# A decode layer with its gradients: the first V window on ScalarE's queue, K windows in slots of their own, the last fill in nested DMAs

## The chip, the core and the metric

The kernel runs on one core of a Trainium2 chip. The metric is the device time of one execution in microseconds; for each kernel the median of its runs is given. Beside the times there is one profiled execution, with a record of every instruction and of every DMA packet. The engines are called by their names or as the profile has them: PE (TensorE), DVE (VectorE), ACT (ScalarE), POOL (GpSimd) and SP (SyncE, which only issues DMAs here). Sixteen DMA engines carry all transfers of the core.

## The reference

One token goes through a pre-norm attention block with a sliding window over a cache and through a bilinear MLP, and then all gradients are taken:

```python
h  = x + attention(layernorm(x), k_cache[..., Sk-W:, :], v_cache[..., Sk-W:, :], wq, wo)
h2 = h + (g * u) @ w_down        # g, u = layernorm(h) @ w_gate, layernorm(h) @ w_up
out, vjp = jax.vjp(f, x, k_cache, v_cache, wq, wo, w_gate, w_up, w_down)
return (out, *vjp(grad_out))
```

Sizes: D = 448, 16 query heads over G = 8 groups of keys and values, head size 256, F = 1792, cache length Sk = 32768, of which the last W = 4096 positions are used. Everything is bfloat16. The gradients of the two caches have the shape of the caches (134 MB each): outside the window they are zero, and these zeros have to be written. That makes 280.59 MB written and 48.33 MB read in one execution.

## The kernel before, in words

The work has three streams.

**Zeros, on SP's queue.** `zeros` is a tile of 128 rows. Sixteen of its rows (`ALL`, rows 32, 36, ..., 92) are the source of every fill, so that each of the sixteen belongs to another DMA engine. `fill` writes a region of HBM from these rows over and over; each descriptor is one row piece of f elements, ZW = 8192 (16 KB) or, for the regions counted in `LONG`, NW = 14336 (28 KB). At first `zeros` holds wq, which the queries need; the first fill therefore comes from another zeroed tile (`odd`, part of `Mt`), and once the queries are done a DMA on ScalarE's queue writes zeros into the sixteen rows (line 110). Then SP issues one fill after another without looking at the compute: regions (0,0) to (7,0) of the two cache gradients (`zero_rows_and_fills`, line 108). The last region, `out_3` of group 7, is cut up by `deal`, which gives some engines more than others: `deal(FILL, 0, 3, 14)` gives 14 pieces of 16 KB to each of the first three rows, `deal_all` gives all sixteen rows the same, and `deal_rest` gives further pieces to POOL's queue in two laps, the first after the forward pass, the second after the last results.

**Loads and results, on POOL's queue.** `BIG` is one tile with nine slots of 16 KB per partition and a tail. A window of K or V of one group (2 MB) fills a slot. V of group g lies in slot g; K goes to slots 7 and 8 in turn (`K_SLOT`). `io_load` keeps the loads in the order in which the program writes them, one behind the other. At the start K0, V0, K1, V1 and V2 are issued; K of group g + 2 is loaded in two halves when group g is done, and V7 in two halves into the slot of K6. The rows x and grad_out (0.9 KB each) come by ScalarE's queue into the first partition of slot 6.

**Compute.** For each group, `scores` (line 363) transposes K on PE by eight tiles of PSUM, copies each to SBUF (`products`, line 346, with `evac`, which takes ScalarE and VectorE in turn) and multiplies by q; `softmax` follows; `moments` (line 393) forms the products of the window that the backward pass needs. The scores of group g + 1 are woven into the moments of group g. After the eight groups come wo, the MLP and its gradients, with the weights loaded by the same queue over the K slots, then `dq` and its broadcast rows. The last stage walks over the eight groups once more, and computes the window's gradients of K and V from small products (line 764), evicts them from PSUM (lines 298 and 300) into a pair of slots, and POOL issues two stores of 2 MB per group (line 789). Behind the last of these come the small pieces of `deal_rest(1)`.

`rows_to_half` (line 231) turns a row of 448 numbers into a tile over partitions by seven casts and small matmuls. `to_rows` (line 561) does the opposite for the rows that are broadcast into `bc2` and `dq_bc`.

Of the kernel before, what the change touches and what calls it, by code (L numbers as in the profile page):

```python
# [8 lines left out]
f32 = mybir.dt.float32  # L9
# [27 lines left out]
TAIL = 9 * SLOT  # L37
RING = TAIL + 6016
SIZE = RING
K_SLOT = [KS + g % 2 for g in range(G)]  # L40


@with_exitstack
def kernel(
# [10 lines left out]

    oT_f = const.tile([128, 32], f32)
    BIG = const.tile([128, SIZE], bf16)
    x_bf = BIG[0:1, 6 * SLOT:6 * SLOT + D]
    S_.dma_start(out=x_bf, in_=A_x.rearrange("a b d -> (a b) d"))
    go_bf = BIG[0:1, 6 * SLOT + 512:6 * SLOT + 512 + D]  # L60
    S_.dma_start(out=go_bf, in_=grad_out.rearrange("a b d -> (a b) d"))

    def flat_rows(w):
# [39 lines left out]
        fill(FILL, last[used[0]:used[0] + 16 * n * f], ALL, n, f)  # L103
        used[0] += 16 * n * f

    LONG = range(6, 11)

    def zero_rows_and_fills():
        f = NW // 4
        S_.dma_start(out=zeros[ALL, :].rearrange("p (n f) -> p n f", f=f), in_=odd[ALL, 0:f].unsqueeze(1).to_broadcast([16, 4, f]))  # L110
        fill(FILL, first[16 * NH * FH:], ALL, (FL - NH * FH) // ZW, ZW)
        for g in range(G):
            for k, o in enumerate((out_2, out_3)):
                if (g, k) not in ((0, 0), (G - 1, 1)):
                    f = NW if 2 * g + k in LONG else ZW
                    fill(FILL, region(o, g), ALL, FL // f, f)
        deal(FILL, 0, 3, 14)
        deal_all(24, ZW)
        deal_all(8, 1224)

    def deal_rest(lap):
        if lap == 0:
            deal(IO, 0, 4, 16, ZL)
            deal(IO, 4, 3, 4, ZL)
            deal(IO, 7, 2, 25, ZL)
            deal(IO, 9, 7, 10, ZL)
        else:
            deal(IO, 0, 5, 2, 512)
            deal(IO, 5, 2, 25)
            deal(IO, 7, 2, 2, 2560)  # L130
            deal(IO, 9, 7, 15)
            assert used[0] == 896 * ZW

    def slot(k):
# [35 lines left out]
    def load_V(g):  # L170
        load_window(Vw[g], A_v_cache, g)

    def load_V_half(g, h):
        t = slice(h * T // 2, (h + 1) * T // 2)
        io_load(Vw[g][:, t, :], A_v_cache[0, g, Sk - W:, :].rearrange("(p t) d -> p t d", t=T)[:, t, :])

    load_K(0)
    load_V(0)
    load_K(1)
    load_V(1)  # L180
    wd_rows = B_w_down.rearrange("(s j m) n -> j s (m n)", s=2, j=128)
    load_V(2)


    ident_bf = const.tile([128, 128], bf16)
# [42 lines left out]
        r0, r1 = i // 2, (7 + i) // 2  # L228
        return row.rearrange("o (m r) -> o m r", r=NI)[:, :, r0:r1 + 1:r1 - r0]

    def rows_to_half(row):
        t = ps.tile([128, NI], f32, tag="tmp", bufs=1)
        for i in range(NI):
            xe = small.tile([1, 128], f32, tag="R", name="xe")
            c = xe[:]
            V_.tensor_copy(out=c.rearrange("o (m r) -> o m r", r=2), in_=half_cols(row, i))  # L236
            P_.matmul(t[:, i:i + 1], lhsT=c, rhs=one[0:1, 0:1], start=True, stop=True)  # L237
        return t

# [56 lines left out]
    def evac(out, in_):  # L296
# [3 lines left out]
            V_.tensor_copy(out=out, in_=in_)  # L300
        evac_ctr[0] += 1

    xX = const.tile([128, NI], f32)
    V_.tensor_copy(out=xX[:], in_=rows_to_half(x_bf)[:])
    rstd1, xh1, xf1, xx1 = layernorm(xX[:], "ln1")


# [35 lines left out]
        pk_ctr[0] += 1  # L343
        return ring(k).rearrange("p (i h d) -> p i h d", i=2, h=2)

    def products(pool, x_at, vecT, g, out_ps, q):
        tr = pool.tile([128, 4, 2, 128], bf16, tag="tr", bufs=2, name="tr")
        for i in range(4):
            for dh in range(2):
                P_.transpose(tr[:, i, dh, :], x_at(g, 4 * q + i)[:, dh * 128:(dh + 1) * 128], ident_bf[:])  # L350
        xt = kt_buf()
        evac(xt, tr[:])
        for i in range(4):
            for dh in range(2):
                P_.matmul(out_ps[:, 4 * q + i, :], lhsT=xt[:, i, dh, :], rhs=vecT[:, 4 * g + dh:4 * g + dh + 3:2],  # L355
                          start=(dh == 0), stop=(dh == 1))
# [6 lines left out]
    def scores(g, q):  # L363
        if q == 0:
            sT[g] = fps.tile([128, T, 2], f32, tag="sT", bufs=2, name="sT")
        products(fps, k_at, qT, g, sT[g], q)

    def softmax(g):
        s = sT[g]
        pmax = small.tile([128, 2], f32, tag="pmax")  # L370
        V_.reduce_max(out=pmax[:], in_=s[:].rearrange("p t h -> p h t"), axis=AX)
        mt = ps.tile([2, 128], f32, tag="tmp", bufs=1)
        P_.transpose(mt[:], pmax[:], ident_f[:])
        gmax = small.tile([2, 1], f32, tag="gmax")
        V_.reduce_max(out=gmax[:], in_=mt[:], axis=AX)
        gd = small.tile([2, 2], f32, tag="gd")
        V_.tensor_scalar(out=gd[:], in0=ident_f[0:2, 0:2], scalar1=gmax[:, 0:1], scalar2=-SCALE, op0=ALU.mult, op1=ALU.mult)
        nb = ps.tile([128, 2], f32, tag="tmp", bufs=1)
        P_.matmul(nb[:], lhsT=one[0:2, 0:1].to_broadcast([2, 128]), rhs=gd[:], start=True, stop=True)
        nbias = small.tile([128, 2], f32, tag="nbias")  # L380
        V_.tensor_copy(out=nbias[:], in_=nb[:])
        e = small.tile([128, T, 2], f32, tag="ef")
        sums = small.tile([128, 2], f32, tag="psums")
        for h in range(2):
            S_.activation(out=e[:, :, h], in_=s[:, :, h], func=ACT.Exp, bias=nbias[:, h:h + 1], scale=SCALE, accum_out=sums[:, h:h + 1])
        rs = small.tile([128, 2], f32, tag="rsum")
        V_.reciprocal(out=rs[:], in_=total(sums[:], 2)[:])
        pf = small.tile([128, T, 2], f32, tag="pp", bufs=2)
        V_.tensor_tensor(out=pf[:], in0=e[:], in1=rs[:].unsqueeze(1).to_broadcast([128, T, 2]), op=ALU.mult)
        V_.tensor_copy(out=pT_all[:, g], in_=pf[:])  # L390
        p_f[g] = pf

    def moments(g):

# [3 lines left out]
        for c in range(T // 2):  # L398
# [16 lines left out]
            if g + 1 < G and 4 <= c < 12:  # L415
                with tc.issue_after(mm.ins):
                    scores(g + 1, c - 4)
                if c == 11:
                    softmax(g + 1)
            if c == 8 and g == G - 2:  # L420
                load_V_half(G - 1, 0)
            if c == 8 and g == G - 1:
                load_wo(0, 9)
        S_.copy(out=Mt[:, g, 0, :], in_=MT[0][:])
# [29 lines left out]

    bc2 = [BIG[:, o:o + F].rearrange("p (i c) -> p i c", i=2) for o in (WD0, WD0 - F)]

    for q in range(8):
        scores(0, q)
    softmax(0)
    for g in range(G):  # L460
        moments(g)
        if g + 2 < G:
            load_K(g + 2, 2)
        if g + 3 < G - 1:
            load_V(g + 3)
        if g == G - 2:
            load_V_half(G - 1, 1)
        if g == 0:

            go_f = BIG[0:1, 6 * SLOT + 1024:6 * SLOT + 1024 + 2 * D].bitcast(f32)  # L470
            V_.tensor_copy(out=go_f, in_=go_bf)
            t = ps.tile([128, D], f32, tag="tmp", bufs=1)
            P_.matmul(t[:], lhsT=one[0:1, 0:1].to_broadcast([1, 128]), rhs=go_f, start=True, stop=True)
            S_.copy(out=dh2_bc[:], in_=t[:])
    load_wo(9, 32)
    io_load(wg_sb, flat_rows(B_w_gate))

# [80 lines left out]
    for w in range(2):  # L558
        V_.tensor_tensor(out=dgu[:, w, 0:FC], in0=d_hh[:], in1=gu[:, 1 - w, :], op=ALU.mult)

    def to_rows(dst, t, cols, j0):
        for j, c in enumerate(cols):
            P_.matmul(t[:, j, :], lhsT=c, rhs=ident_bf[:, j0:j0 + t.shape[-1]], start=True, stop=True)
        evac(dst, t)

    P2 = const.tile([128, 2, NI], f32)
    for w, w_sb in ((0, wg_sb), (1, wu_sb)):
        for h in range(4):
            r = small.tile([2, HF // 4], bf16, tag="R", name="r")
            t = ps.tile([2, NI, 32], f32, tag="tmp", bufs=1, name="t")  # L570
            to_rows(r[:].rearrange("s (j m) -> s m j", m=NI), t[:], [dgu[:, w, m::NI] for m in range(NI)], 32 * h)
            for i2 in range(2):
                bc = ps.tile([128, HF // 4], f32, tag="tmp", bufs=1, name="bc")
                P_.matmul(bc[:], lhsT=Par[:, i2:i2 + 128], rhs=r[:], start=True, stop=True)
                evac(bc2[w][:, i2, h * HF // 4:(h + 1) * HF // 4], bc[:])
        wv = w_sb.rearrange("p (i c) -> p i c", i=NI)
        for i in range(NI):
            V_.tensor_tensor_reduce(out=wv[:, i, :], in0=wv[:, i, :], in1=bc2[w][:, i % 2, :], scale=1.0, scalar=0.0,
                                    op0=ALU.mult, op1=ALU.add, accum_out=P2[:, w, i:i + 1])
    dhn = const.tile([128, NI], f32)  # L580
# [7 lines left out]
    for b in range(32):  # L588
        V_.tensor_tensor_reduce(out=wg_sb[:, 0:D], in0=parked.get(b, wo_b(b)), in1=dh_bc[:], scale=1.0, scalar=0.0,  # L589
                                op0=ALU.mult, op1=ALU.add, accum_out=doW[:, b:b + 1])  # L590
    doT_f = small.tile([128, 32], f32, tag="pp", bufs=2, name="doT_f")
    V_.tensor_copy(out=doT_f[:], in_=regroup(doW[:], 1)[:])
    doT = const.tile([128, 32], bf16)
# [25 lines left out]
    rows16(doT, do_rows, 1.0)  # L619
    for b1 in range(0, 16, 4):  # L620
        r = wg_sb[0:2, b1 * 128:b1 * 128 + 512]
        t = ps.tile([2, 4, 128], f32, tag="tmp", bufs=1, name="t")
        to_rows(r.rearrange("s (b c) -> s b c", c=128), t[:], [dq[:, b:b + 17:16] for b in range(b1, b1 + 4)], 0)
        for i2 in range(2):
            bc = ps.tile([128, 512], f32, tag="tmp", bufs=1, name="bc")
            P_.matmul(bc[:], lhsT=Par[:, i2:i2 + 128], rhs=r, start=True, stop=True)
            evac(dq_bc[:, i2, b1 * 128:b1 * 128 + 512], bc[:])
    load_odd(IO)
# [92 lines left out]
    def dP(s, q):  # L721
        g = SEQ[s]
        if q == 0:
            dps[s] = bps.tile([128, T, 2], f32, tag="dp", name="dp")
        products(bps, v_at, doT, g, dps[s], q)

    def factors(s):
        R_ps = ps.tile([128, 2 * Dh], f32, tag="tmp", bufs=1)
# [94 lines left out]
```

## Time and profile before

| what | value |
|---|---|
| median of 3 runs | 777.7 us (776.77 to 778.44) |
| profiled execution | 777.6 us, its span 775.8 us |
| PE busy | 468.8 us (60%) |
| VectorE busy | 394.3 us (51%) |
| ScalarE busy | 155.5 us (20%) |
| POOL busy | 42.2 us (5%) |
| mean granted TensorE clock | 0.665 |
| moved by DMA | 330.09 MB |

Busy shares of compute engines are averages over the span. The span is also cut into 40 equal slices of 19.4 us, with a digit for the busy share in tenths, and a line for the DMA engines together. DMA queues are listed by the bytes they moved and by the share of the sixteen engines' time that their packets took. A view by stretches gives, for any cut of the span, each engine's busy time with the number of instructions, the granted clock, the DMA share and GB/s. The DMA share can pass 1 by a little, since packets overlap by a few nanoseconds.

The stages lie like this: the first scores from 18 us, the moments of the eight groups from 41 to 246 us, some 26 us each; wo and the MLP to 335; gradients of the MLP to 407; the last stage to 702.

### The profile page before, as it was taken

Reading aid. Unit: us, or ns where it says so; the run is one execution under the profiler, and the core shown is the slowest. Engines: PE = TensorE matmul, PEld = TensorE weight load, DVE = VectorE, ACT = ScalarE, POOL = GpSimd, SP = SyncE. Lnnn points to the kernel's source line nnn. Section 1 sums busy time; section 2 is a strip of 40 time slices with the busy share of each in tenths; the row PEclk is TensorE's granted clock in tenths of the full one; section 3 lists DMA queues with packets and bytes.
Section 4 is the critical chain, followed back from the end, with each engine's and each line's share of the span. In section 5 each row is a group of like instructions: output and inputs, shape, how many; then the busy total and the mean of one; then the engine's idle time right before and its main releaser. Section 6 shows DMA issues by size and latency. Waiting matters only on the chain. (4 is left out here: it accounts for less than half of the span.)

```text
span 775.8 us, 10948 instructions
## 1 busy us (share of the span) xinstructions
PE 468.8 (60%) x4427; PEld 259.6 (33%) x4472; DVE 394.3 (51%) x1179; ACT 155.5 (20%) x268; POOL 42.2 (5%) x86
## 2 busy tenths in 40 slices
PE   3899998998996423041326839686958977360000
PEld 2755565555553121020323414232313333030000
DVE  5277766766774121146683526464646756980000
ACT  0211222122110000021003414243423433130000
POOL 2000000000000000010001000000000100001000
PEclk9999999999999755555555555555555555555555
DMA  9999999999999999999999999999999999999998
GB/s 362 429 426 429 425 427 429 427 425 427 428 424 429 433 428 430 436 437 430 427 432 428 431 428 433 428 429 424 432 430 429 431 428 429 429 430 432 431 429 349
DMA packets 22803, 330.09 MB, mean 425 GB/s; under 512 B 2717, under 2 KB 2719, under 8 KB 3992
## 3 DMA queue, kind: packets, MB, share of 16 engines
q1 hardware_dynamic: 12701, 231.17, 69.6%
q0 software_dynamic: 9968, 97.77, 29.9%
q8 instruction: 35, 0.57, 0.3%
q10 hardware_dynamic: 84, 0.46, 0.1%
q14 instruction: 15, 0.12, 0.0%
HBM read 48.33 MB, written 280.59 MB: 424 GB/s over the span
## 5 line engine op out<-in xcount | busy, mean ns | idle before, releaser
L764 PE MATMUL d_ps<-BIG 32*128 32x512 bf16 x256 | 121.4, 598 | 60.2 <-ACT BIG L298 42.8
L407 PE MATMUL MT<-BIG 128*128 128x512 bf16 x467 | 134.5, 394 | 3.8 <-DMA BIG<-in_A_v_cache_dram 1.9
L403 DVE TENSOR_SCALAR BIG<-BIG,pf 128x256 bf16<-128x256 bf16 x512 | 112.6, 280 | 29.9 <-PE MT L407 25.2
L350 PE MATMUL tr<-ident_bf,BIG 128*128 128x128 bf16 x1024 | 113.5, 269 | 20.1 <-DVE doW L589 12.6
L298 ACT CAST BIG<-d_ps 128x512 bf16<-128x512 f32 x156 | 88.4, 588 | 176.8 <-PE d_ps L764 128.3
L350 PEld LDWEIGHTS <-BIG 128*128 128x128 bf16 x1024 | 81.1, 120 | 51.9 <-issue 44.1
L300 DVE COPY BIG<-tr 128x1024 bf16<-128x1024 bf16 x92 | 63.3, 688 | 50.7 <-PE tr L350 50.6
L300 DVE CAST BIG<-d_ps 128x512 bf16<-128x512 f32 x100 | 67.9, 683 | 34.8 <-DMA out_dram<-BIG 28.1
L298 ACT COPY BIG<-tr 128x1024 bf16<-128x1024 bf16 x36 | 36.4, 1012 | 131.6 <-PE tr L350 116.3
L355 PEld LDWEIGHTS <-BIG 128*128 128x128 bf16 x1024 | 36.7, 102 | 70.7 <-DVE BIG L300 44.2
L410 PEld LDWEIGHTS <-BIG 128*128 128x128 bf16 x512 | 42.1, 98 | 44.2 <-issue 8.3
L410 PE MATMUL acc<-pT_all,BIG 128*128 128x2 bf16 x512 | 44.9, 164 | 7.9 <-DVE kbar L427 6.2
L764 PEld LDWEIGHTS <-BIG 32*128 32x128 bf16 x256 | 20.7, 111 | 78.4 <-issue 59.2
L407 PEld LDWEIGHTS <-BIG 128*128 128x128 bf16 x512 | 39.0, 100 | 21.0 <-issue 8.6
L413 PE MATMUL acc<-pT_all,BIG 128*128 128x2 bf16 x512 | 44.2, 164 | 0.0
L413 PEld LDWEIGHTS <-BIG 128*128 128x128 bf16 x512 | 29.9, 96 | 0.9
L528 DVE CUSTOM_DVE_ANT_0 dh_bc<-BIG,dh_bc 128x448 bf16<-128x448 bf16 x14 | 8.7, 624 | 40.5 <-DMA BIG<-in_B_w_down_dram 40.2
L355 PE MATMUL dp<-doT,BIG 128*128 128x2 bf16 x512 | 24.2, 168 | 4.3 <-DVE BIG L300 3.4
L549 PE MATMUL y<-BIG,hh_bf 128*1 128x448 bf16 x14 | 5.9, 564 | 31.5 <-DMA BIG<-in_B_w_down_dram 30.8
L355 PE MATMUL sT<-qT,BIG 128*128 128x2 bf16 x512 | 22.1, 164 | 0.8 <-ACT BIG L298 0.6
L745 DVE TENSOR_TENSOR BIG<-r_ps,mrow 96x1024 bf16<-96x1024 bf16 (+2 forms) x15 | 18.3, 1221 | 1.0 <-PE r_ps L750 0.8
L237 PE MATMUL t<-one,xe 1*128 1x1 f32 x42 | 11.2, 333 | 12.6 <-DVE xe L236 12.6
(190 smaller groups left out, 357.4 us busy)
## 6 DMA issues: line engine op xcount, KB each, us to landing
out_dram<-zeros SPq DMA_DIRECT2D x14, 14336.0 KB, 160.5
out_dram<-BIG POOLq DMA_DIRECT2D x17, 2048.0 KB, 32.4
BIG<-in_A_v_cache_dram POOLq DMA_DIRECT2D x8, 2048.0 KB, 25.2
BIG<-in_A_k_cache_dram POOLq DMA_DIRECT2D x12, 1024.0 KB, 15.0
out_dram<-zeros SPq DMA_DIRECT2D x1, 11264.0 KB, 45.3
out_dram<-zeros SPq DMA_DIRECT2D x1, 6144.0 KB, 81.3
BIG<-in_A_k_cache_dram POOLq DMA_DIRECT2D x2, 2048.0 KB, 24.9
zeros<-in_A_wq_dram SPq DMA_DIRECT2D x1, 3584.0 KB, 15.3
```

Of the source, the lines that this page charges most:

```text
L237: P_.matmul(t[:, i:i + 1], lhsT=c, rhs=one[0:1, 0:1], start=True, stop=True)
L298: S_.copy(out=out, in_=in_)
L300: V_.tensor_copy(out=out, in_=in_)
L350: P_.transpose(tr[:, i, dh, :], x_at(g, 4 * q + i)[:, dh * 128:(dh + 1) * 128], ident_bf[:])
L355: P_.matmul(out_ps[:, 4 * q + i, :], lhsT=xt[:, i, dh, :], rhs=vecT[:, 4 * g + dh:4 * g + dh + 3:2], start=(dh == 0), stop=(dh == 1))
L403: V_.tensor_scalar(out=pk[:, i, h, :], in0=K[:, t, :], scalar1=pf[:, t, h:h + 1], scalar2=None, op0=ALU.mult)
L407: P_.matmul(MT[hf][:], lhsT=v_at(g, t)[:, hf * 128:(hf + 1) * 128], rhs=pk[:, i, :, :].rearrange("p h d -> p (h d)"), start=(t == 0), stop ...
L410: P_.matmul(acc[:, 2 * hf:2 * hf + 2], lhsT=v_at(g, t)[:, hf * 128:(hf + 1) * 128], rhs=pT_all[:, g, t, :], start=(t == 0 and hf == 0), st ...
L413: mm = P_.matmul(acc[:, 4 + dk:7 + dk:2], lhsT=K[:, t, dk * 128:(dk + 1) * 128], rhs=pT_all[:, g, t, :], start=False, stop=(t == T - 1), s ...
L528: V_.tensor_tensor_reduce(out=dh_bc[:], in0=wd_sb[:, m - m0, :], in1=dh2_bc[:], scale=1.0, scalar=0.0, op0=ALU.mult, op1=ALU.add, accum_ou ...
L745: V_.tensor_tensor(out=rows[p0:p1], in0=r_ps[p0:p1, :].unsqueeze(1).to_broadcast([p1 - p0, 8, 128]), in1=mrow[p0:p1, :].unsqueeze(2).to_br ...
L764: mm = P_.matmul(d_ps[:].rearrange("p w d -> p (w d)"), lhsT=rows[32 * k:32 * k + 32, a, :], rhs=R[32 * k:32 * k + 32, :], start=True, sto ...
```

## The change

K gets slots 3 to 8 for groups 0 to 5, and 7 and 8 again for groups 6 and 7. K0 to K5 are loaded whole; K6, K7 and V7 come in halves, the first in the middle of the moments of groups 4, 5 and 6 and the second behind them (`LATE`). V0 leaves POOL's queue and is issued on ScalarE's, behind the fifth of the seven copies of the x row, which moves from VectorE to ScalarE for it. POOL's queue begins with K0, K1, V1, K2, and goes on with V2, K3 and K4 after the first layer norm's part of the program. The rows x and grad_out lie in slot 8 instead of 6; K5 is loaded there once grad_out's row has been used.

On the fill side one more region has 28 KB pieces; the last fill of SP, eight pieces of 1224 elements for all rows, becomes four of 1658 elements for all rows and then fifteen DMAs over 15, 14, ..., 1 rows, each with one piece of 256 + 16k elements for k rows. Pieces of POOL's second lap become larger and fewer.

On the compute side the eight evictions per group in `scores` all go to ScalarE (before: in turn), and so do those of `bc2[1]`; the products with the gate and up weights are walked in reverse order; `dq`'s broadcast gets a PSUM pool of its own with two and four buffers in place of the single `tmp` buffer.

```diff
-K_SLOT = [KS + g % 2 for g in range(G)]
+K_SLOT = [3, 4, 5, 6, 7, 8, 7, 8]
...
-    x_bf = BIG[0:1, 6 * SLOT:6 * SLOT + D]
+    x_bf = BIG[0:1, 8 * SLOT:8 * SLOT + D]
...
-    LONG = range(6, 11)
+    LONG = range(5, 11)
...
         deal_all(24, ZW)
-        deal_all(8, 1224)
+        deal_all(4, 1658)
+        for k in range(15, 0, -1):
+            deal(FILL, 0, k, 1, 256 + 16 * k)
...
             deal(IO, 0, 5, 2, 512)
-            deal(IO, 5, 2, 25)
+            deal(IO, 5, 2, 16, 12800)
             deal(IO, 7, 2, 2, 2560)
-            deal(IO, 9, 7, 15)
+            deal(IO, 9, 7, 10, ZL)
...
+    def load_V0():
+        S_.dma_start(out=Vw[0], in_=A_v_cache[0, 0, Sk - W:, :].rearrange("(p t) d -> p t d", t=T))
+
+    def load_half(dst, cache, g, h):
         t = slice(h * T // 2, (h + 1) * T // 2)
+        io_load(dst[:, t, :], cache[0, g, Sk - W:, :].rearrange("(p t) d -> p t d", t=T)[:, t, :])
...
     load_K(0)
-    load_V(0)
     load_K(1)
     load_V(1)
...
-    load_V(2)
+    load_K(2)
...
-    def rows_to_half(row):
+    def rows_to_half(row, meanwhile=None):
...
+            if meanwhile and i == 4:
+                turned = S_.copy(out=c.rearrange("o (m r) -> o m r", r=2), in_=half_cols(row, i))
+                with tc.issue_after(turned.ins):
+                    meanwhile()
+            else:
+                V_.tensor_copy(out=c.rearrange("o (m r) -> o m r", r=2), in_=half_cols(row, i))
...
+    def on_act(out, in_):
+        S_.copy(out=out, in_=in_)
...
-    V_.tensor_copy(out=xX[:], in_=rows_to_half(x_bf)[:])
+    V_.tensor_copy(out=xX[:], in_=rows_to_half(x_bf, load_V0)[:])
...
-        products(fps, k_at, qT, g, sT[g], q)
+        products(fps, k_at, qT, g, sT[g], q, on_act)
...
+    LATE = {4: (Kw[6], A_k_cache, 6), 5: (Kw[7], A_k_cache, 7), 6: (Vw[7], A_v_cache, 7)}
...
-            if c == 8 and g == G - 2:
-                load_V_half(G - 1, 0)
+            if c == 8 and g in LATE:
+                load_half(*LATE[g], 0)
...
+    load_V(2)
+    load_K(3)
+    load_K(4)
     for q in range(8):
         scores(0, q)
     softmax(0)
     for g in range(G):
         moments(g)
-        if g + 2 < G:
-            load_K(g + 2, 2)
-        if g + 3 < G - 1:
+        if g < 4:
             load_V(g + 3)
-        if g == G - 2:
-            load_V_half(G - 1, 1)
+        if g in LATE:
+            load_half(*LATE[g], 1)
         if g == 0:
...
             S_.copy(out=dh2_bc[:], in_=t[:])
+            load_K(5)
...
-    for w, w_sb in ((0, wg_sb), (1, wu_sb)):
+    for w, w_sb, ev in ((0, wg_sb, evac), (1, wu_sb, on_act)):
...
-        for i in range(NI):
+        for i in reversed(range(NI)):
...
+    tps_cm.__exit__(None, None, None)
+    tps_cm = tc.tile_pool(name="qps", bufs=1, space=bass.MemoryType.PSUM)
+    tps = tps_cm.__enter__()
...
-        t = ps.tile([2, 4, 128], f32, tag="tmp", bufs=1, name="t")
+        t = tps.tile([2, 4, 128], f32, tag="qt", bufs=2, name="t")
...
-            bc = ps.tile([128, 512], f32, tag="tmp", bufs=1, name="bc")
+            bc = tps.tile([128, 512], f32, tag="qb", bufs=4, name="bc")
```

More of the change, by code (lines that the diff above doesn't have):

```diff
@@ L57 @@
     BIG = const.tile([128, SIZE], bf16)
-    x_bf = BIG[0:1, 6 * SLOT:6 * SLOT + D]
+    x_bf = BIG[0:1, 8 * SLOT:8 * SLOT + D]
     S_.dma_start(out=x_bf, in_=A_x.rearrange("a b d -> (a b) d"))
-    go_bf = BIG[0:1, 6 * SLOT + 512:6 * SLOT + 512 + D]
+    go_bf = BIG[0:1, 8 * SLOT + 512:8 * SLOT + 512 + D]
     S_.dma_start(out=go_bf, in_=grad_out.rearrange("a b d -> (a b) d"))
@@ L171, in load_V @@
         load_window(Vw[g], A_v_cache, g)
-    def load_V_half(g, h):
+    def load_V0():
+        S_.dma_start(out=Vw[0], in_=A_v_cache[0, 0, Sk - W:, :].rearrange("(p t) d -> p t d", t=T))
+    def load_half(dst, cache, g, h):
         t = slice(h * T // 2, (h + 1) * T // 2)
-        io_load(Vw[g][:, t, :], A_v_cache[0, g, Sk - W:, :].rearrange("(p t) d -> p t d", t=T)[:, t, :])
+        io_load(dst[:, t, :], cache[0, g, Sk - W:, :].rearrange("(p t) d -> p t d", t=T)[:, t, :])
     load_K(0)
-    load_V(0)
     load_K(1)
@@ L235, in rows_to_half @@
             c = xe[:]
-            V_.tensor_copy(out=c.rearrange("o (m r) -> o m r", r=2), in_=half_cols(row, i))
+            if meanwhile and i == 4:
[4 more added lines that the diff above has]
+                V_.tensor_copy(out=c.rearrange("o (m r) -> o m r", r=2), in_=half_cols(row, i))
             P_.matmul(t[:, i:i + 1], lhsT=c, rhs=one[0:1, 0:1], start=True, stop=True)
@@ L344, in pk_buf, with products @@
         return ring(k).rearrange("p (i h d) -> p i h d", i=2, h=2)
-    def products(pool, x_at, vecT, g, out_ps, q):
+    def products(pool, x_at, vecT, g, out_ps, q, ev):
         tr = pool.tile([128, 4, 2, 128], bf16, tag="tr", bufs=2, name="tr")
@@ L351, in products @@
         xt = kt_buf()
-        evac(xt, tr[:])
+        ev(xt, tr[:])
         for i in range(4):
@@ L461 @@
         moments(g)
-        if g + 2 < G:
-            load_K(g + 2, 2)
-        if g + 3 < G - 1:
+        if g < 4:
             load_V(g + 3)
-        if g == G - 2:
-            load_V_half(G - 1, 1)
+        if g in LATE:
+            load_half(*LATE[g], 1)
         if g == 0:
-            go_f = BIG[0:1, 6 * SLOT + 1024:6 * SLOT + 1024 + 2 * D].bitcast(f32)
+            go_f = BIG[0:1, 8 * SLOT + 1024:8 * SLOT + 1024 + 2 * D].bitcast(f32)
             V_.tensor_copy(out=go_f, in_=go_bf)
@@ L559, with to_rows @@
         V_.tensor_tensor(out=dgu[:, w, 0:FC], in0=d_hh[:], in1=gu[:, 1 - w, :], op=ALU.mult)
-    def to_rows(dst, t, cols, j0):
+    def to_rows(dst, t, cols, j0, ev=evac):
         for j, c in enumerate(cols):
             P_.matmul(t[:, j, :], lhsT=c, rhs=ident_bf[:, j0:j0 + t.shape[-1]], start=True, stop=True)
-        evac(dst, t)
+        ev(dst, t)
     P2 = const.tile([128, 2, NI], f32)
-    for w, w_sb in ((0, wg_sb), (1, wu_sb)):
+    for w, w_sb, ev in ((0, wg_sb, evac), (1, wu_sb, on_act)):
         for h in range(4):
@@ L570 @@
             t = ps.tile([2, NI, 32], f32, tag="tmp", bufs=1, name="t")
-            to_rows(r[:].rearrange("s (j m) -> s m j", m=NI), t[:], [dgu[:, w, m::NI] for m in range(NI)], 32 * h)
+            to_rows(r[:].rearrange("s (j m) -> s m j", m=NI), t[:], [dgu[:, w, m::NI] for m in range(NI)], 32 * h, ev)
             for i2 in range(2):
@@ L574 @@
                 P_.matmul(bc[:], lhsT=Par[:, i2:i2 + 128], rhs=r[:], start=True, stop=True)
-                evac(bc2[w][:, i2, h * HF // 4:(h + 1) * HF // 4], bc[:])
+                ev(bc2[w][:, i2, h * HF // 4:(h + 1) * HF // 4], bc[:])
         wv = w_sb.rearrange("p (i c) -> p i c", i=NI)
-        for i in range(NI):
+        for i in reversed(range(NI)):
             V_.tensor_tensor_reduce(out=wv[:, i, :], in0=wv[:, i, :], in1=bc2[w][:, i % 2, :], scale=1.0, scalar=0.0,
@@ L724, in dP @@
             dps[s] = bps.tile([128, T, 2], f32, tag="dp", name="dp")
-        products(bps, v_at, doT, g, dps[s], q)
+        products(bps, v_at, doT, g, dps[s], q, evac)
     def factors(s):
```

## The prediction

> **What bounds the kernel now.** I read the slices of the span first, with the DMA line, then the DMA queues, then the end of the span in stretches of 1 us, then the engines' last instructions, and last the groups of instructions in the stages that the change touches.
>
> ```profile
> PEclk9999999999999755555555555555555555555555
> DMA  9999999999999999999999999999999999999998
> GB/s 362 429 426 429 425 427 429 427 425 427 428 424 429 433 428 430 436 437 430 427 432 428 431 428 433 428 429 424 432 430 429 431 428 429 429 430 432 431 429 349
> DMA packets 22803, 330.09 MB, mean 425 GB/s; under 512 B 2717, under 2 KB 2719, under 8 KB 3992
> ...
> q1 hardware_dynamic: 12701, 231.17, 69.6%
> q0 software_dynamic: 9968, 97.77, 29.9%
> ```
>
> The DMA engines are full in every slice but the first and the last, at 424 to 437 GB/s, whatever the compute engines do. So the time is bytes divided by rate, plus what is lost at the two ends. q1 is SP's queue (the zero fills), q0 is POOL's (loads and results).
>
> ```profile
> 770.00:771.00 1.00, 0.00 (x0) 0.00 (x0) 0.00 (x0) 0.00 (x0) 0.00 (x0) 0.50 0.89 382
> 771.00:772.00 1.00, 0.00 (x0) 0.00 (x0) 0.00 (x0) 0.00 (x0) 0.00 (x0) 0.50 0.82 342
> 772.00:773.00 1.00, 0.00 (x0) 0.00 (x0) 0.00 (x0) 0.00 (x0) 0.00 (x0) 0.50 0.45 182
> 773.00:774.00 1.00, 0.00 (x0) 0.00 (x0) 0.00 (x0) 0.00 (x0) 0.00 (x0) 0.50 0.21 83
> 774.00:775.00 1.00, 0.00 (x0) 0.00 (x0) 0.00 (x0) 0.00 (x0) 0.00 (x0) 0.50 0.03 10
> 775.00:775.80 0.80, 0.00 (x0) 0.00 (x0) 0.00 (x0) 0.00 (x0) 0.00 (x0) 0.50 0.00 0
> ```
>
> The last two columns are the DMA share and GB/s. The sixteen engines run out one by one. The trace's packet records (queue, size, start and duration of each DMA packet; no line of the page lists them) date the sixteen completions of the last fill: 767.1, then 771.6 to 774.5, mean 772.5. The last engine ends 2.0 us after the mean, and 1.3 us later the span ends. It is one of the first three engines: its completion of the 14-packet deal (759.1) is one of the three that exist for that deal, and 24 packets and the last eight follow without a gap.
>
> ```profile
> 699.24 1.08 POOL L789 DMA_DIRECT2D out_dram<-BIG  x2 [5.34 <-issue]
> 700.32 2.44 POOL L89 DMA_DIRECT2D out_dram<-zeros  x4
> ...
> 692.71 38.27 SPq L89 DMA_DIRECT2D out_dram<-zeros  x2
> ...
> 702.00:741.00 39.00, 0.00 (x0) 0.00 (x0) 0.00 (x0) 0.00 (x0) 0.75 (x2) 0.50 1.01 430
> ```
>
> Compute is over at 702.8, while the engines stay full for 68 us more. By the packet records 22.9 MB of SP's and 7.3 MB of POOL's queue are still unsent at 702. SP's stream alone lasts 22.9 MB / 430 GB/s = 53 us, so compute could end some 50 us later before an engine had nothing to do, and a faster compute frees nothing. SP issues its last DMA by 731.0 (692.71 + 38.27), 43 us ahead of its end.
>
> **The change, part by part.** Bytes stay as they are: each window of K and V is read as often as before, and each fill is re-cut to the same sum (128 x 1224 = 64 x 1658 + the sum of k(256 + 16k) for k = 1 to 15 = 156,672 elements; 25 x 8192 = 16 x 12800; 15 x 8192 = 10 x 12288). What changes is packets, order and balance. In the records, packets of 16,384 B follow each other on one engine every 607.5 ns, those of 2,448 B every 95.4 ns: 5.6 ns per packet and 36.7 ns per 1000 B. A completion of 4 B takes 5.5 ns of an engine.
>
> K of groups 2 to 5 comes whole: 512 packets of 16 KB instead of 1,024 of 8 KB. The line gives 512 x 5.6 / 16 = 0.18 us; the undisturbed durations (2 x 309 - 611 = 7 ns, less 3.5 ns of overlap) give 0.11, the mean ones (2 x 314 - 617 = 11 ns) 0.35. I take -0.2.
>
> One more region in 28 KB packets: 512 instead of 896, 384 x 5.6 / 16 = -0.13 us (-0.12 by mean durations of 613 and 1069 ns). The second lap of deals has 9 packets fewer on two engines and 5 fewer on seven: at most 0.05 us each, and none on the first three, so 0.
>
> The last fill: each engine had 8 x 95.4 = 763 ns. Now four packets of 3,316 B take 4 x 127.3 = 509. If, as in the deal of three rows, k rows go to the first k engines, the first engine adds 15 packets with 11,520 B in all (423 + 84 ns) and 15 completions (83 ns): 1,099, or +0.34 us. The third adds 13 (10,400 B): +0.27. The sixteenth adds none: -0.25. Where one of the first three ends last, as here, this costs +0.3; where the sixteenth does, it gains 0.25. I take +0.3. SP has fifteen DMAs more to issue. Its unblocked issues took 0.39 to 0.65 us, so at most 15 x 0.65 = 9.8 us, hidden by the 43 us by which SP is ahead; without that cover all 9.8 would show.
>
> V of group 0 moves from POOL's queue, second place, to ScalarE's, behind a copy. It is past K1, V1 and K2 then, and K1 and V1 start one place earlier. Nothing depends on an empty engine here: four loads of 2 MB lie in POOL's queue from the start, three more behind the masks. Queued behind it on ScalarE's ring is the DMA that rewrites the zero rows (issued 23.6, landed 33.2), which SP's fills wait for; the fill before them lasts to 38.7, and longer with a third queue beside it, so the cover is 5 us, and past it the loads alone keep the engines full. The copy on ScalarE takes the place of a 0.21 us cast. What it does to the rate is not shown before, since no stage has three full queues. The excess of packet durations over the median of their kind, summed and divided by 16, is 0.8 us in the stretch around 10 to 30 us, where these loads run: between all of it gained and as much lost, -0.8 to +0.8. The nearest rows, loads beside fills from 66 on, run at 424 to 431 GB/s like the rest, so I take 0.
>
> K in slots of its own, score evictions and those of bc2[1] on ScalarE, the new PSUM pool, the reversed order: all compute. Of the eight evictions per group four move.
>
> ```profile
> L298 ACT COPY BIG<-tr 128x1024 bf16<-128x1024 bf16 x36 | 36.4, 1012 | 131.6 <-PE tr L350 116.3
> ...
> L300 DVE COPY BIG<-tr 128x1024 bf16<-128x1024 bf16 x92 | 63.3, 688 | 50.7 <-PE tr L350 50.6
> ```
>
> That is 32 x 0.688 = 22 us off VectorE and 32 x 1.012 = 32 us onto ScalarE, which idles. K6 and K7 now load in halves while group 4 and 5 run, and may come late. Even all 32 us on the path stay below the 50 us of cover; without it they would show in full. So 0.
>
> **Sum**, against the profiled execution's own 777.6 (span 775.8 and 1.8 around it; the median of the runs, 777.7, is 0.1 above): -0.2 - 0.13 + 0.3 + 0 = about 0, and with half of the tail's cost in doubt -0.1 to -0.2: **777.4**. Its own range adds the bounds, -0.35 - 0.15 - 0.25 - 0.8 = -1.55 and -0.11 - 0.12 + 0.34 + 0.8 = +0.9, to 776.1 to 778.5. Runs shown spread over 1.7 us, so 0.2% (1.55 us) is about what can be told from no change.
>
> **Rivals.**
>
> *Ends and contention improve (faster).* The excess durations sum to 4.4 us, about 2.2 of it between 10 and 230 us, where windows are read beside fills; the tail wastes 2.0. Fewer, larger reads that come early might save half of the first (1.1), the staircase half of the second (1.0), packets 0.35: 777.6 - 2.45 = **775.2**. For it: 8 KB reads carry 0.6 us of that excess. Against: the staircase loads just the engines that end late in this profile.
>
> *The nested DMAs wait for their completions (slower).* Place: the last fifteen fills, on the first engine. If each completion held the ring until its data had landed, the price is the 1.3 us from the last packet (774.5) to the end of the span: 14 x 1.3 = 18 us, **796**. It decides from 1.6 / 14 = 0.11 us each. Against: in the records the packet behind a completion starts 5 to 6 ns after it, also at the last boundary. But no row shows completions 40 ns apart on one ring. The Trainium skill (DMA: Bandwidth & Descriptors, sections Anatomy of one DMA — SWDGE (gpsimd) path and Rules for kernel authors) speaks against this edit: each DMA costs about 2.0 us fixed, and below 64 KB one pays mostly overhead. Taken serially, that is an estimate of 15 x 2.0 = 30 us, some 807; the trace's 5 to 6 ns at a boundary disagrees, though not for DMAs this small.
>
> *The rows aren't spread as meant (slower).* If all 120 rows (101,120 B) went through one engine: 3.7 + 0.67 us, less the 0.25 it saves, +4.1: **781.7**. Against: the deal of three rows completed on three engines.
>
> *Three queues disturb the start (slower).* +0.8, and K0 and the zero rows later, the same again: **779.2**.
>
> **How the numbers follow.** Forecast 0.52, the gain 0.30, completions 0.09, one engine 0.03, disturbed start 0.06. Of the forecast some 0.04 is measured as faster, 0.02 as slower; half of the last rival stays within 0.2%. So faster 0.34, same 0.50, slower 0.16. The range reaches to the gain and takes in the disturbed start: 775.1 to 779.6; what lies beyond it, the other slower cases and the ends of the gain, is below 0.2.
>
> **What would show it.** DMA packets near 21,970 (22,803 - 512 - 384 - 53 + 56 + 120 completions, less some 64 for fewer POOL loads); the DMA line unbroken at 424 to 437 GB/s; in the tail the first engines 0.3 us later against the others; POOL's last issue moved by up to some 20 us without an effect on the end. I am wrong if the last engine's lag of 2.0 us changes by more than 1 us, if a slice in the middle falls below 420 GB/s, or if the stretch after the last wide fill grows by several us.

## The result: 0.74% slower, and the profile after

The changed kernel takes 783.19 us (median of 6 runs, 782.95 to 783.8) against 777.43 us for the kernel before (6 runs beside it, 776.77 to 778.44). The ratio is 1.0074, with a 95% interval of 1.0061 to 1.0087. The profiled execution took 782.95 us with a span of 781.1, 5.3 more than before. The forecast was 777.4, at most 779.6.

The page of the changed kernel, its slices and packet count:

```profile
DMA  9999999999999999999999999999999999999995
GB/s 369 422 427 428 426 427 428 427 429 426 427 428 430 428 437 427 436 430 433 430 432 426 434 426 434 430 427 429 426 431 431 428 430 428 430 431 429 431 433 223
DMA packets 21796, 330.10 MB, mean 423 GB/s; under 512 B 2602, under 2 KB 2724, under 8 KB 3933
```

Thirty-eight slices are as full as before. Only the last one differs: 223 GB/s in place of 349. So nothing was lost on the way. The end of the span in stretches of 2 us (the last two columns are the DMA share and GB/s):

```profile
770.00:772.00 2.00, 0.00 (x0) 0.00 (x0) 0.00 (x0) 0.00 (x0) 0.00 (x0) 0.50 0.86 356
772.00:774.00 2.00, 0.00 (x0) 0.00 (x0) 0.00 (x0) 0.00 (x0) 0.00 (x0) 0.50 0.18 65
774.00:776.00 2.00, 0.00 (x0) 0.00 (x0) 0.00 (x0) 0.00 (x0) 0.00 (x0) 0.50 0.03 9
776.00:778.00 2.00, 0.00 (x0) 0.00 (x0) 0.00 (x0) 0.00 (x0) 0.00 (x0) 0.50 0.01 4
778.00:780.00 2.00, 0.00 (x0) 0.00 (x0) 0.00 (x0) 0.00 (x0) 0.00 (x0) 0.50 0.01 3
```

By the packet records the engines are done with all that has been issued at 773.4; before, the last completion of a fill came at 774.5. Then six microseconds follow in which they move next to nothing. The timeline of SP's queue says what they wait for (start, time until the last of the group is issued, number of DMAs):

```profile
734.64 3.93 SPq L89 DMA_DIRECT2D out_dram<-zeros  x3
...
758.20 2.02 SPq L89 DMA_DIRECT2D out_dram<-zeros  x2
...
773.01 6.27 SPq L89 DMA_DIRECT2D out_dram<-zeros  x9
```

SP stops twice, and issues the last nine of the fifteen nested DMAs only from 773.01 on, one every 0.70 us (6.27 / 9). Its list of waits (in total, how many, the longest) has an entry at line 89 that the kernel before does not have; there SP waits for fills only at the close of the program, line 818. First after, then before:

```profile
SPq L89 <- DMA out_dram<-zeros: 32.4, 2, 19.6
```

```profile
SPq L818 <- DMA out_dram<-zeros: 43.4, 3, 38.4
```

So in the changed kernel SP waits 32.4 us, in two waits, for the landing of an earlier fill. Which fill it is can be read in the program's instruction list for SP, with the semaphore that each DMA waits for (a semaphore is a counter that a DMA raises when its data has landed; number 19, 384 pieces of 8192, is the wide fill, and number 21 the first nested DMA):

```
18 L89 DMACopy out_dram<-zeros 42x1x8192 [waits DMAHW5_49]
19 L89 DMACopy out_dram<-zeros 384x1x8192 [waits DMAHW6_49]
20 L89 DMACopy out_dram<-zeros 64x1x1658 [waits DMAHW7_49]
21 L89 DMACopy out_dram<-zeros 15x496 [waits DMAHW0_49]
...
25 L89 DMACopy out_dram<-zeros 11x432 [waits DMAHW4_49]
26 L89 DMACopy out_dram<-zeros 10x416 [waits DMAHW5_49]
27 L89 DMACopy out_dram<-zeros 9x400 [waits DMAHW6_49]
28 L89 DMACopy out_dram<-zeros 8x384 [waits DMAHW7_49]
```

Eight semaphores serve SP's DMAs in turn, so each of these DMAs waits for the completion of the one eight places ahead of it. With fills of 14 MB that is far in the past. Number 25 waits for the last whole region (17), number 26 for the 14-packet deal (18), number 27 for the wide fill (19), the last large piece of work there is. The trace's completion records agree to 0.02 us: the semaphore of number 17 gets its last count at 758.18 and number 25 starts at 758.20; that of number 19 gets its last at 773.00 and number 27 starts at 773.01. The first stop costs nothing by itself, since the engines are still full. At the second the wide fill has just landed, and nine issues are still to come.

### The profile page after: what moved, and what is told of

Its sections match the earlier page's. It is cut to its first block, busy times and chain, and to the rows that moved or that the text cites. A ratio compares the mean times of both kernels' runs of the same rounds, so it can differ in the third digit from the quotient of the medians.

```text
span 781.1 us, 11055 instructions
## 1 busy us (share of the span) xinstructions
PE 472.6 (61%) x4472; PEld 262.2 (34%) x4472; DVE 373.8 (48%) x1140; ACT 192.9 (25%) x308; POOL 39.3 (5%) x81
## 2 busy tenths in 40 slices
DMA packets 21796, 330.10 MB, mean 423 GB/s; under 512 B 2602, under 2 KB 2724, under 8 KB 3933
## 5 line engine op out<-in xcount | busy, mean ns | idle before, releaser
L421 PE MATMUL MT<-BIG 128*128 128x512 bf16 x512 | 144.8, 395 | 3.8 <-DMA BIG<-in_A_v_cache_dram 3.8
L417 DVE TENSOR_SCALAR BIG<-BIG,pf 128x256 bf16<-128x256 bf16 x512 | 114.3, 284 | 57.3 <-PE MT L421 53.7
L362 PE MATMUL tr<-ident_bf,BIG 128*128 128x128 bf16 x1024 | 116.1, 268 | 6.2 <-DMA BIG<-in_A_k_cache_dram 5.1
L362 PEld LDWEIGHTS <-BIG 128*128 128x128 bf16 x1024 | 81.2, 120 | 46.8 <-issue 39.8
L313 ACT COPY BIG<-tr 128x1024 bf16<-128x1024 bf16 x64 | 64.6, 1012 | 109.6 <-PE tr L362 105.5
L424 PEld LDWEIGHTS <-BIG 128*128 128x128 bf16 x512 | 44.7, 99 | 51.5 <-issue 10.9
L309 DVE COPY BIG<-tr 128x1024 bf16<-128x1024 bf16 x60 | 41.2, 687 | 40.8 <-PE tr L362 40.8
L367 PEld LDWEIGHTS <-BIG 128*128 128x128 bf16 x1024 | 37.0, 102 | 65.7 <-DVE BIG L309 32.4
L421 PEld LDWEIGHTS <-BIG 128*128 128x128 bf16 x512 | 39.2, 99 | 21.3 <-issue 7.2
L427 PEld LDWEIGHTS <-BIG 128*128 128x128 bf16 x512 | 30.0, 96 | 0.9
```

The lines of the kernel that those rows point to most:

```text
L313: S_.copy(out=out, in_=in_)
L417: V_.tensor_scalar(out=pk[:, i, h, :], in0=K[:, t, :], scalar1=pf[:, t, h:h + 1], scalar2=None, op0=ALU.mult)
L421: P_.matmul(MT[hf][:], lhsT=v_at(g, t)[:, hf * 128:(hf + 1) * 128], rhs=pk[:, i, :, :].rearrange("p h d -> p (h d)"), start=(t == 0), stop ...
L424: P_.matmul(acc[:, 2 * hf:2 * hf + 2], lhsT=v_at(g, t)[:, hf * 128:(hf + 1) * 128], rhs=pT_all[:, g, t, :], start=(t == 0 and hf == 0), st ...
L427: mm = P_.matmul(acc[:, 4 + dk:7 + dk:2], lhsT=K[:, t, dk * 128:(dk + 1) * 128], rhs=pT_all[:, g, t, :], start=False, stop=(t == T - 1), s ...
```

## The experiments

All medians are in us; "before" is the kernel before in the same batch, and the ratio is to it, with its 95% interval.

| run | median | before | ratio |
|---|---|---|---|
| e1, single last fill in the changed kernel | 777.27 | 777.83 | 0.9994 [0.9986, 1.0003] |
| e2, nested fill alone in the kernel before | 783.61 | 777.83 | 1.0072 [1.0056, 1.0087] |
| e3, ten nested DMAs | 780.81 | 777.83 | 1.0037 [1.0023, 1.0051] |
| e4, the fifteen spread among the large fills | 777.65 | 777.83 | 1.0002 [0.9994, 1.0011] |
| e5, six nested DMAs | 778.11 | 777.82 | 1.0007 [0.9998, 1.0016] |
| e6, more 28 KB packets and a sixteenth row with more | 788.80 | 777.82 | 1.0139 [1.0121, 1.0156] |
| e7, more 28 KB packets alone | 782.59 | 777.94 | 1.0058 [1.0044, 1.0073] |
| e8, the sixteenth row with more, alone | 786.35 | 777.94 | 1.0101 [1.0085, 1.0118] |
| e9, single last fill and `LONG` of before | 776.78 | 777.82 | 0.9985 [0.9976, 0.9994] |
| e10, e9 with less on the first three engines | 776.73 | 777.82 | 0.9985 [0.9976, 0.9995] |

### e1 and e2: the part undone, and the part alone

e1, against the changed kernel:

```diff
-        deal_all(4, 1658)
-        for k in range(15, 0, -1):
-            deal(FILL, 0, k, 1, 256 + 16 * k)
+        deal_all(8, 1224)
```

> The changed kernel with the last fill of before (eight pieces of 1224 elements, one DMA) in place of the nested ones; all else as changed. Theory (a DMA of SP waits for the completion of the eighth DMA before it, so nine of the nested ones are issued one by one at 0.70 us after the last wide fill has landed): the whole loss goes and what the rest of the change is worth shows, 783.2 - 9 x 0.70 - 0.5 = 776.4, some 1.0 below before. Rival (loads and compute cost the time): 782 or more. Rival (the small DMAs cost by their number): about 777.4, as before.

e2 is the reverse edit in the kernel before.

> The kernel before with only the last fill changed to four pieces of 1658 and the fifteen nested DMAs. Theory: +6 to +7, 783.5 to 784.5, with two waits of SP of some 13 and 20 us and nine issues after the last wide fill has landed. Rival (loads and compute cost the time): 777.5.

e1 gives 777.27 and e2 783.61: the last fill alone carries the loss, and loads, slots and compute edits carry none of it that can be told. In e2's timeline SP stops in the same way:

```profile
774.68 6.27 SPq L89 DMA_DIRECT2D out_dram<-zeros  x9
```

The same nine DMAs and the same 6.27 us, in a kernel whose loads and compute are those of before. The guess of a full 1.0 us gain for the rest was not met: e1's interval includes no change. (The part on e9 shows where that gain went.)

### e3, e4 and e5: how many, and where

e3 and e5 keep ten and six nested DMAs with the same bytes:

```diff
-        deal_all(4, 1658)
-        for k in range(15, 0, -1):
-            deal(FILL, 0, k, 1, 256 + 16 * k)
+        deal_all(4, 1608)                 # e5: deal_all(4, 1623)
+        for k in range(15, 5, -1):        # e5: range(15, 9, -1)
+            deal(FILL, 0, k, 1, 512)      # e5: 704
```

> The changed kernel with ten nested DMAs (15 to 6 rows, 512 elements each) and four pieces of 1608. Same bytes. Theory: six can be issued before the last wide fill has landed, so four are late instead of nine: 783.2 - 5 x 0.70 = 779.7. Rival (a price for each nested DMA): two thirds of the loss, 781.3.

> The changed kernel with six nested DMAs (15 to 10 rows, 704 elements each) and four pieces of 1623. Theory: the last of the six waits for the 14-packet deal only, which has landed some 14 us before the end, so no issue is late and nothing is lost: 777.3, as with the single last fill, and no issue of SP behind 765. Rival (a price for each nested DMA, 5.9 us / 15 = 0.39 each): 779.6.

e4 keeps all fifteen, but puts one behind each large fill:

```diff
                     fill(FILL, region(o, g), ALL, FL // f, f)
+                    r = 16 - 2 * g - k
+                    deal(FILL, 0, r, 1, 256 + 16 * r)
+        deal(FILL, 0, 1, 1, 256 + 16)
         deal(FILL, 0, 3, 14)
         deal_all(24, ZW)
         deal_all(4, 1658)
-        for k in range(15, 0, -1):
-            deal(FILL, 0, k, 1, 256 + 16 * k)
```

> The changed kernel with the same fifteen small DMAs, but one behind each of the region fills (the last before the deal), and the four pieces of 1658 as the last DMA. Theory: every DMA's eighth predecessor has landed long before, so no issue is late: 776.4. Rival (small DMAs, their packets or their completions, are dear on the first engines): 783, as changed.

e3's timeline of SP's queue at the end:

```profile
773.76 2.98 SPq L89 DMA_DIRECT2D out_dram<-zeros  x4
```

Four late issues, as the semaphore count says. e3's 780.81 lies 1.1 above what was expected, and on the side of the rival's 781.3. The time alone does not decide there. Nor do the steps: no late DMA 778.11 (e5), four 780.81, nine 783.19, so 2.7 us for the first four (0.68 each, and 2.98 us of issuing in the timeline) and 2.4 for the next five; but in these three kernels the late ones are always the nested ones less six, so a price for each nested DMA could rise in the same way. What speaks against such a price is e5 by itself, 1.5 below the 779.6 that it would give, and above all e4. In e5 the last issue is far from the end:

```profile
758.48 2.18 SPq L89 DMA_DIRECT2D out_dram<-zeros  x2
```

and e4, with all fifteen small DMAs and their completions, takes 777.65, and its interval includes no change. Its theory had 776.4, too low by the same guess of a gain as e1's. So neither the number of small DMAs nor their packets cost the time. What costs it is standing at the end of a queue in which the eighth predecessor is the last large transfer. In e4 SP's list shows no wait for a fill at line 89. In e5 it shows the first of the two stops, 19.4 us, and that stop alone costs nothing that can be told.

### e6, e7 and e8: a version that was to be better, and was worse

With the loss settled, I tried to go below both kernels by fewer packets and by work for the sixteenth engine. In the changed kernel's packet records one engine ends its four pieces of the last fill at 766.9, 4 us ahead of the next, and has no packet of the fifteen-row DMA behind them; so I took it for the engine of the sixteenth row.

```diff
-    LONG = range(5, 11)
+    LONG = range(1, 11)                   # e6 and e7
...
+        deal_all(4, 1424)                 # e6 and e8, the last fill (e7: deal_all(8, 1224))
...
-            deal(IO, 9, 7, 10, ZL)        # e6 and e8, second lap
+            deal(IO, 9, 6, 10, ZL)
+            deal(IO, 15, 1, 23)
```

> The changed kernel with one last fill (four pieces of 1424), four more regions in 28 KB packets (LONG from 1 to 10), and 65,536 elements moved from the last fill of all sixteen rows to the sixteenth row, in POOL's second lap, since the sixteenth engine ended 5 us before the others. Theory (the time is DMA work over sixteen engines, plus the tail): 4 x 384 x 5.6 / 16 = 0.54 us less from packets, 0.3 less from the tail, 777.3 - 0.84 = 776.4. Rival (loads share the rings with larger fill packets, come later, and compute ends later by more than its cover): 778 or more.

> The changed kernel with the single last fill of before and LONG from 1 to 10 (four more regions in 28 KB packets). Theory (larger fill packets take ring turns from POOL's loads, compute ends some 27 us later as in the run before, and POOL's second lap of pieces, which few engines carry, comes when SP's stream is nearly dry): 784 to 788. Rival (that loss came from the fifth deal on POOL's queue for the sixteenth row): 776.8.

> The changed kernel with one last fill (four pieces of 1424) and the 65,536 elements for the sixteenth row in POOL's second lap, LONG as changed. Theory (compute's lateness made the loss of the run with both): 777.3 - 0.3 = 777.0. Rival (the fifth deal is issued late, behind a completion on POOL's queue, and the sixteenth engine ends last): 780 or more.

e6 has both parts and takes 788.80; alone, e7 takes 782.59 and e8 786.35. Both halves lose, and for different reasons. In e7 the end of the span looks like this:

```profile
765.00:770.00 5.00, 0.00 (x0) 0.00 (x0) 0.00 (x0) 0.00 (x0) 0.00 (x0) 0.50 0.99 424
770.00:775.00 5.00, 0.00 (x0) 0.00 (x0) 0.00 (x0) 0.00 (x0) 0.00 (x0) 0.50 0.57 238
775.00:780.00 5.00, 0.00 (x0) 0.00 (x0) 0.00 (x0) 0.00 (x0) 0.00 (x0) 0.50 0.05 18
```

Its timeline of POOL has the last four deals 25.5 us later than e1's (709.41 there):

```profile
734.90 2.34 POOL L89 DMA_DIRECT2D out_dram<-zeros  x4
```

And its list of waits on SP shows the close of the program (line 835):

```profile
SPq L835 <- PEq L835: 3.1, 2, 2.6
```

Where both queues have work, the packet records, chained by end and start, show load and fill packets one by one in turn on each engine (254 to 262 us in e1, 272 to 280 in e7). So a longer fill packet makes each load wait longer: from issue to landing the first part of `wo` (2576 KB) takes 22.1 us instead of 16.5 in e1, the gate weights 34.8 instead of 26.7, and compute ends later. POOL's second lap, whose large pieces nine rows carry, then meets a stream of fills that is nearly dry: the last packet is at 777.1 instead of 773.6 in e1.

POOL's own queue now ends last, level with SP's, and the close takes 4.1 us behind the last packet, where it takes 2.0 in e1 and 1.3 before; the wait above is 1.4 in e1 and 0.7 before. The list puts that wait down to PE, but the records of POOL show what came last: its closing DRAIN instruction ends at 780.41, 3.3 us behind the last packet of POOL's queue (777.12), and the span ends 0.8 us later. In all twelve profiles this DRAIN ends 3.2 to 3.4 us behind POOL's last packet. So the 5.5 us by which the span of e7 is longer than that of e1 are 3.5 us of tail and 2.0 of close. That fewer engines carry the tail is my reading of the first part; no run separates it.

In e8 compute is on time, but the engines slow down while still busy:

```profile
755.00:760.00 5.00, 0.00 (x0) 0.00 (x0) 0.00 (x0) 0.00 (x0) 0.00 (x0) 0.50 1.05 407
760.00:765.00 5.00, 0.00 (x0) 0.00 (x0) 0.00 (x0) 0.00 (x0) 0.00 (x0) 0.50 0.95 326
```

A share of 0.95 with 326 GB/s means long packets. The packet records have the 23 pieces of the one-row deal: ten of them took 1.4 to 4.9 us instead of 0.61, and several ran at once (4.24 us from 758.60, 2.02 from 759.08, 3.57 from 759.57). At 762.05 five of them run at once, among 15 packets in all. From 30 us to the end the records of e8, of e1 and of the kernel before never have more than sixteen packets of data at once, apart from overlaps under 20 ns, which is one for each engine; so these were on several engines: the deal of a single row was not taken by the engine of that row, as the edit meant, but spread. That they were slow because all read the same row of the tile is my inference; no run here separates it. The rival was right in that the fifth deal did the harm, but not in how: the deal is issued late (722.10), yet POOL's queue ends at 773.2 and the last packet, at 781.0, is one of SP's.

### e9 and e10: below the kernel before

```diff
-    LONG = range(5, 11)
+    LONG = range(6, 11)
...
-        deal(FILL, 0, 3, 14)              # e10 only
+        deal(FILL, 0, 3, 13)
-        deal_all(4, 1658)
-        for k in range(15, 0, -1):
-            deal(FILL, 0, k, 1, 256 + 16 * k)
+        deal_all(8, 1224)                 # e10: 1416
```

> The changed kernel with the last fill and LONG (6 to 10) of before; the V0 queue, the K slots and the compute edits stay. Theory (the extra 28 KB region takes ring turns from the weight loads, so compute ends some 8 us later than before, POOL's queue ends 2.6 us later, and its end at the close of the program costs what the packets saved): compute ends near 702 again and 0.4 to 0.6 comes off, 776.8. Rival (the loads' new order itself makes compute late): POOL's last issue still near 711, and 777.4.

> As the run before it, and one 16 KB piece less on each of the first three engines, spread over all sixteen in the last fill (1416 elements instead of 1224). Theory (one of the first three engines ends last): another 0.3 to 0.5 off, 776.4. Rival (which engine ends last is chance): no difference, 776.8.

e9 is faster than the kernel before by 0.15%, and its interval stays below 1. In its profile POOL's deals come 4.4 us earlier than in e1 (and still 4.7 later than before, so the new order of the loads or the compute edits delay them too),

```profile
705.00 2.35 POOL L89 DMA_DIRECT2D out_dram<-zeros  x4
```

POOL's last completion is at 764.1 instead of 771.6, and the wait at the close is small again (e1 had 1.4 there):

```profile
SPq L835 <- PEq L835: 0.6, 2, 0.5
```

The intervals of e1 and e9 overlap, so that `LONG` costs half a microsecond is likely rather than shown; the move of POOL's end is in the traces. They also show where e1's gain went: SP's last packet ends 0.8 us earlier in e1 than before (773.6 against 774.5), but POOL's DRAIN ends at 774.9, and the span is only 0.2 shorter (775.7 against 775.8). In e9 the DRAIN ends at 767.3, SP's last packet at 773.4, and the span is 1.1 shorter than before.

e10's theory fell: one packet less on the first three engines changes nothing (776.73 against 776.78). The rival, that it is chance which engine ends last, fits this, but is not shown by itself.

## Why the prediction was wrong, step by step

**The step that failed** is the cover given to SP's issues: "SP has fifteen DMAs more to issue. Its unblocked issues took 0.39 to 0.65 us, so at most 15 x 0.65 = 9.8 us, hidden by the 43 us by which SP is ahead; without that cover all 9.8 would show." The lead of 43 us belonged to a queue with few, large DMAs. It was read off a timeline, without asking what allows SP to be ahead. Each DMA waits for the eighth before it, and with fifteen small ones behind the wide fill that wait reaches the wide fill itself. The price of an issue was nearly right, 0.70 us: nine of them from 773.01 on take 6.27, and the last completion of SP's fills moved from 774.5 to 779.8, the 5.3 us by which the span grew. The prediction's own sign of being wrong, a stretch behind the last wide fill that grows by several us, came true: from the wide fill's last count to the end of the span it is 1.8 us before (774.05 to 775.83) and 8.1 after.

The wait could have been looked for. The kernel before has twenty DMAs on SP and shows no wait of line 89 for a fill; that no wait shows says nothing of a queue with fifteen more.

**The rival of the nested DMAs** was at the right place, with a chance of 0.09, but its mechanism was another one. It let completions hold the ring on the engine's side, 1.3 us for each of fourteen. The traces show SP's queue held instead, only for nine, and at the cost of an issue. The Trainium skill (DMA: Bandwidth & Descriptors, section Anatomy of one DMA — SWDGE (gpsimd) path) says that DMA engines do not wait on semaphores and that any such wait happens on the issuing sequencer before dispatch; the trace agrees, with nine issues between 773.01 and 779.28 and engines at 3 to 9 GB/s from 774 on. Its 2.0 us per DMA, fitted there to DMAs that POOL issues, did not appear as a price of each of SP's: that was 0.70 per late DMA, and none that can be told where the DMA was early (e4).

**The other rivals** did not come true. The rows were spread as meant: the nine packets of number 27 start within 0.06 us of each other (774.39 to 774.45), so they were not on one engine. Of the gain of 2.5 us e1, which has all of the change but the nested fill, could show all but the 1.0 of the staircase, and the disturbed start of 1.6 us in full; its interval, 1.1 us faster to 0.2 slower, leaves out both.

**The bound** was right: the DMA line is unbroken and the time is DMA work plus the ends. **The packets** were about right: the durations in the records sum to 775.81 us per engine before and 775.33 after, 0.48 less, against 0.33 forecast; 21,796 packets against 21,970. **V on ScalarE's queue** took 0 of the range's 0.8 either way, as far as e1 can tell. **The staircase** of +0.3, the smaller pieces and their completions, could not be told apart from chance; e5 and e4, which have such pieces, lie 0.8 and 0.4 above e1, inside what their intervals allow.

**Compute costs nothing** was right in the outcome and wrong in its size. POOL's last issue moved by 8 us without a loss that can be told, but the cover is not 50 us: e7 ends compute 25 us later than e1 and loses 5 us. The 53 us counted bytes over all engines, and left out the close: POOL's queue ended at 769.0 before, its DRAIN 3.4 us later, and 0.8 us are needed behind that, which leaves an estimated 2.6 us to the end of the span at 775.8. e1's POOL queue ends 2.5 us later than that and has used them up.

## What to carry to other kernels

How far a queue runs ahead depends on what its next DMA waits for. Before adding small transfers to the end of a queue, find out how many places back each one waits for a completion (here eight, so that seven could follow the wide fill without waiting for it), and put no more of them behind the last large transfer; the same small transfers cost nothing that can be told among the large ones. A cover in microseconds holds for the queue as it is: recount it by engine and by queue when the order changes.

## What the runs showed of the hardware

- An issue on SP takes 0.70 us for DMAs of nine rows and fewer when they follow each other with idle engines (6.27 us for nine, the last 0.42); that made most of the 5.8 us lost.
- A POOL DMA from one row, with 23 pieces of 16 KB, ran on several engines at once, ten of its packets at 1.4 to 4.9 us instead of 0.61 (e8).
- POOL's closing DRAIN ends 3.2 to 3.4 us behind the last packet of POOL's queue, in all twelve profiles, and the span ends 0.8 us later where this DRAIN comes last (e1, e6, e7). Where SP's last packet is late enough, as before and in e9, the span ends 1.3 us behind it.
- With work in both queues, load and fill packets take turns one by one on an engine (e1, e7), so the size of a fill's pieces sets how long a load takes: 16.5 us for the first part of `wo` in e1, 22.1 in e7.
